# The token half of a Fourier mix as four 32-row products of even and odd tokens

## The chip, the cores and the metric

One core of a Trainium2 chip runs the whole kernel. The metric is the time on the device in microseconds; the median of several runs counts. Everything is float32.

## The reference

Attention inside chunks of 64 tokens, then a Fourier mix over tokens and channels, and a two-layer MLP on the normed sum:

```python
# q, k, v: (8, 8, 576, 64); chunk = 64
attn = softmax(q_c @ k_c.T / 8)            # in each of the 9 chunks of a head
x = (attn @ v_c) -> (8, 576, 512)          # heads side by side
mixed = real(fft(fft(x, axis=1), axis=2))  # over 576 tokens, then 512 channels
u = x + mixed
un = (u - mean(u)) / sqrt(var(u) + 1e-6)   # over the channels
out = u + relu(un @ w_ch1) @ w_ch2         # 512 -> 2048 -> 512; weights in float64
```

## The kernel before

**Tiles.** The 9 chunks of a batch of 576 tokens are held in tiles of 128 rows: `lo` tiles (chunks 0 to 3, tokens turned round), `hi` tiles (chunks 8 to 5, in mirrored order beside them), and a `rest` tile with chunk 4 of two batches, 64 rows each. NM = 2 pairs of lo and hi tiles, NQ = 289 outputs of the token transform, HQ = 128 channels, CH = 64.

**The mix.** The transform of a real signal folds in both directions. `fold` (L491) adds mirrored tokens (lo + hi) and mirrored channels, and leaves in `pm` four blocks T of 128 channels for each pair and a `pm_rest` for chunk 4, with one more column for the middle channel (L528). `fourier` (L644) then does the token half: `product` (L650) multiplies each block by the table `tk` (cosine or sine) into four PSUM tiles `z` (two of the pool `ps_t`, two called `more_z` of `ps_a`). For each T there are two products over 128 rows and one over 64 rows (`pm_rest`), each 289 columns wide, and twelve of one row of output for the middle channel. ACT copies the outputs to `zf` (tokens 0 to 255) and `zr` (the rest, mirrored; L678 to L688). `mixed` (L691) does the channel half with the tables ce, co, cx, so; `both` and `added` put the result back into the token tiles, mirrored. Batch 0 has its own `fourier_early` (L727), and `turn_tables` (L248) makes its tables in the wanted order from those in `start`.

**Order.** The order on each engine is written by hand. The main loop (L1212 to L1246) runs the MLP of group g as a generator (`mlp`, L1133): `up` steps and then `down` steps, each of 4 matmuls of 512 columns or 8 to 16 of 256. After each step t it advances the side work of the next batch, `attention(b)`, PAUSE = 3 empty steps, and `fourier(b)` (L1186). How many side steps are due is worked out from `sizes` (L1196), so that the batch is ready when its own MLP begins:

```python
due = min(sizes[cur], (t - t0) * sizes[cur] // (t1 - t0))
while done < due:
    heavy = next(sides[cur], None) or heavy
```

If no side step was `heavy`, `round_next` turns a piece of the weights from float64 to float32 on DVE and ACT (`round_weight`, L287), in group 0 only. `keep2` and `keep1` (L905, L888) then form sums of weight blocks on DVE and POOL and write them to DRAM (`s1`, `s2`), from where `fetch` (L926) brings them back for `up_halves` and `down_halves`. `operands` (L937) forms sums of h1.

**Queues.** SP issues nearly all DMAs in the order of the program: weights, q, k, v, the parts of s1 and s2, `shift` (L477: it moves single rows between tiles), and `store` (L871), which writes a finished tile to `out`.

Of the kernel before, what the change touches and what calls it, by code (L numbers as in the profile page):

```python
# [16 lines left out]
def kernel(  # L17
# [67 lines left out]
    tk = const.tile([128, NM + 1, 2, NQ], FP32, name="tk")  # L85
# [84 lines left out]
    more_v = one_p.tile([128, 4 * NL + 64], FP32, tag="zf", name="more_v")  # L170
# [53 lines left out]
    def load_tables():  # L224

        t = start[:, 0:(NM + 1) * 2 * NQ].rearrange("p (i r f) -> p i r f", i=NM + 1, r=2)
        for c in range(2 * NM):  # L230
            (i, r0), (j, p0) = divmod(c * CH, 128), divmod((NC - 1 - c) * CH, 128)
            nc.sync.dma_start(out=t[r0:r0 + CH, i], in_=seq_tab[p0:p0 + CH, j])
        for r0 in (0, CH):
            nc.sync.dma_start(out=t[r0:r0 + 1, NM], in_=seq_tab[0:1, 0])
            nc.sync.dma_start(out=t[r0 + 1:r0 + CH, NM], in_=seq_tab[1:CH, NM])
        for i in range(2):
            nc.sync.dma_start(out=first_rest[32 + 32 * i:33 + 32 * i, 0:DM], in_=dim_tab[0:1, 1 + 2 * i, :])
# [9 lines left out]

    def turn_tables():  # L248
        t = start[:, 0:(NM + 1) * 2 * NQ]
        a, b = tk.rearrange("p i r f -> p (i r) f"), t.rearrange("p (i f) -> p i f", f=NQ)  # L250
        for c in range(2 * NM):
            nc.scalar.copy(a[:, :, c * CH:(c + 1) * CH], b[:, :, (c + 1) * CH:c * CH:-1])
        nc.scalar.copy(a[:, :, NL:NL + 1], b[:, :, 0:1])
        nc.scalar.copy(a[:, :, NL + 1:NQ], b[:, :, NL + 1:NQ])
# [157 lines left out]
    def att_P(n):  # L412
        ex = es.pop(n)
        pt = turn(lambda j: ex[:, j].rearrange("p e k -> p (e k)"))
        t = one_p.tile([128, NJ, 128], FP32, tag="pT", name="pT")
        nc.scalar.copy(t, pt)
        pT[n] = t
# [45 lines left out]

    def shift_early(i):

        lows = [xt(at[LO, 0, j])[:, 0:DM] for j in range(NM)]
        rest, kept = xt(rests[0])[0:1, 0:DM], first_rest[0:1, 0:DM]
        if i == 0:
            nc.gpsimd.tensor_copy(kept, lows[1][0:1])
            nc.gpsimd.tensor_copy(lows[1][0:1], lows[1][CH:CH + 1])  # L470
            nc.gpsimd.tensor_copy(lows[1][CH:CH + 1], rest)
        else:
            nc.scalar.copy(rest, lows[0][0:1])
            nc.scalar.copy(lows[0][0:1], lows[0][CH:CH + 1])
            nc.scalar.copy(lows[0][CH:CH + 1], kept)

    def shift(b):  # L477

        lows = [xt(at[LO, b, i]) for i in range(NM)]
        r = b % 2 * CH  # L480
# [3 lines left out]
        for i in range(NM):  # L484
            eng.dma_start(out=t[2 * i:2 * i + 2, 0:DM], in_=lows[i][0:CH + 1:CH, 0:DM])
        eng.dma_start(out=t[2 * NM:2 * NM + 1, 0:DM], in_=rest)
        for i in range(NM):
            eng.dma_start(out=lows[i][0:CH + 1:CH, 0:DM], in_=t[2 * i + 1:2 * i + 3, 0:DM])
        eng.dma_start(out=rest, in_=t[0:1, 0:DM])

    def fold(b, i):  # L491
# [7 lines left out]
        if i < NM:  # L499
            pm = two_p.tile([128, DM + 1], FP32, tag="pm", name="pm")  # L500
# [5 lines left out]
        else:  # L506
            pm = two_p.tile([128, 2 * HQ + 1], FP32, tag="pm_rest", name="pm_rest")
# [10 lines left out]
        if i < NM:  # L518
# [3 lines left out]
            to = pm[:, 3 * HQ:DM + 1:HQ]  # L522
        else:
            for T, op in enumerate((ALU.add, ALU.subtract, ALU.subtract, ALU.add)):
                to = pm[T % 2 * CH:T % 2 * CH + CH, T // 2 * HQ:T // 2 * HQ + HQ]
                eng.tensor_tensor(out=to, in0=near[:, T // 2], in1=far[:, T // 2], op=op)
            to = pm[CH:, HQ:2 * HQ + 1:HQ]
        eng.tensor_copy(to, two[p, HM + 1 + HQ:HQ - 1:-HM - 1])  # L528
        pms[b, i] = pm

    def attention_early():
# [33 lines left out]
        turn_tables()  # L565
# [77 lines left out]

    def fourier(b):  # L644
        h = b % 2
        zf = one_p.tile([128, 4 * NL + 64], FP32, tag="zf", name="zf")
        zf = zf[:, 0:4 * NL].rearrange("p (t f) -> p t f", t=4)
        pm = [pms.pop((b, i)) for i in range(NM + 1)]

        def product(T, i, out_, lhsT, start, stop, cols=slice(0, NQ)):  # L650
            p = slice(0, 128) if i < NM else slice(T % 2 * CH, T % 2 * CH + CH)
            nc.tensor.matmul(  # L652
                out=out_, lhsT=lhsT[p], rhs=tk[p, i, T // 2 if T != 5 else 0, cols],
                start=start, stop=stop, skip_group_check=True,
            )


        z = [ps_t.tile([128, 512], FP32, tag="pt", name="z") for _ in range(2)]
        more = ps_a.tile([128, 2, 512], FP32, tag="att", name="more_z")
        z += [more[:, k] for k in range(2)]  # L660
        for T in range(4):
            for i in range(NM):
                product(T, i, z[T][:, 0:NQ], pm[i][:, T * HQ:(T + 1) * HQ], i == 0, False)
            if T == 1:
                yield
        for T in range(4):
            product(T, NM, z[T][:, 0:NQ], pm[NM][:, T // 2 * HQ:(T // 2 + 1) * HQ], False, True)

        mids = []
        for g, c0 in enumerate(range(0, NQ, NS)):  # L670
            c1 = min(c0 + NS, NQ)
            mids.append((c0, c1, z[2][32 * g:32 * g + 1, NQ:NQ + c1 - c0]))
        for i in range(NM + 1):
            for c0, c1, out_ in mids:
                one = pm[i][:, DM:DM + 1] if i < NM else pm[i][:, 2 * HQ:2 * HQ + 1]
                product(5, i, out_, one, i == 0, i == NM, slice(c0, c1))
        for T in range(4):
            nc.scalar.copy(zf[:, T, :], z[T][:, 0:NL])  # L678
            nc.scalar.copy(zr[:, T, h, 0:NQ - NL], z[T][:, NL:NQ])
            upper, mirrored = zr[:, T, h, NQ - NL:CH], z[T][:, NQ - 2:NL:-1]  # L680
            nc.scalar.activation(out=upper, in_=mirrored, func=ACTF.Copy, scale=1.0 if T < 2 else -1.0)
            for c0, c1, from_ in mids if T == 2 else ():
                n = max(0, min(c1, NL) - c0)
                if n > 0:
                    nc.scalar.copy(zf[0:1, T, c0:c0 + n], from_[:, 0:n])
                if c1 > NL:
                    nc.scalar.copy(zr[0:1, T, h, 0:NQ - NL], from_[:, n:])
                    nc.scalar.copy(zr[0:1, T, h, NQ - NL:CH], from_[:, NQ - 2 - c0:NL - c0:-1])  # L688
        yield
# [37 lines left out]
    def fourier_early():  # L727
# [3 lines left out]
        zf = one_p.tile([128, 4 * NL + 64], FP32, tag="zf", name="zf")  # L731
# [6 lines left out]
        mids = [(c0, min(c0 + NS, NQ)) for c0 in range(0, NQ, NS)]  # L738
        order = (1, 0, NM)
        for i in order:  # L740
            at_ = {"start": i == order[0], "stop": i == order[-1], "skip_group_check": True}
            for T in range(4):
                p = slice(0, 128) if i < NM else slice(T % 2 * CH, T % 2 * CH + CH)
                d0_ = T * HQ if i < NM else T // 2 * HQ
                nc.tensor.matmul(out=z[T][:, 0:NQ], lhsT=pm[i][p, d0_:d0_ + HQ], rhs=tk[p, i, T // 2], **at_)
            p, d0_ = (slice(0, 128), DM) if i < NM else (slice(CH, 128), 2 * HQ)
            for r, (c0, c1) in enumerate(mids):
                nc.tensor.matmul(
                    out=mid[32 * r:32 * r + 1, 0:c1 - c0], lhsT=pm[i][p, d0_:d0_ + 1], rhs=tk[p, i, 0, c0:c1], **at_
                )  # L750
        for T in range(4):
            if T % 2:
                nc.vector.tensor_copy(zf[:, T, :], z[T][:, 0:NL])
            else:
                nc.scalar.copy(zf[:, T, :], z[T][:, 0:NL])
        for r, (c0, c1) in enumerate(mids):
            n, from_ = min(c1, NL) - c0, mid[32 * r:32 * r + 1]
            if r % 2:
                nc.vector.tensor_copy(zf[0:1, 2, c0:c0 + n], from_[:, 0:n])
            else:  # L760
                nc.scalar.copy(zf[0:1, 2, c0:c0 + n], from_[:, 0:n])
        round_weight(1, put_off, "h")
        for T in range(4):
            nc.scalar.copy(zr[:, T, 0, 0:NQ - NL], z[T][:, NL:NQ])
            upper, mirrored = zr[:, T, 0, NQ - NL:CH], z[T][:, NQ - 2:NL:-1]
            nc.scalar.activation(out=upper, in_=mirrored, func=ACTF.Copy, scale=1.0 if T < 2 else -1.0)
            if T == 2:
                n = NL - c0
                nc.scalar.copy(zr[0:1, T, 0, 0:NQ - NL], from_[:, n:c1 - c0])
                nc.scalar.copy(zr[0:1, T, 0, NQ - NL:CH], from_[:, NQ - 2 - c0:n:-1])  # L770
# [100 lines left out]
    def store(n, o):  # L871

        if kind(n) == LO:
            b, c = chunks(n)[0]
            to = out[b, c * CH + 1:c * CH + 129, :].rearrange("(c p) d -> c p d", c=2)
            nc.sync.dma_start(out=to[:, ::-1], in_=o)
            return
        for h, (b, c) in enumerate(chunks(n)):
            r0, t0 = h * CH, c * CH
            if kind(n) == RE:  # L880
                eng = nc.scalar if n in groups[-1][1::2] and h else nc.sync
                eng.dma_start(out=out[b, t0 + 1:t0 + CH, :], in_=o[r0 + 1:r0 + CH])
                eng.dma_start(out=out[b, 0:1, :], in_=o[r0:r0 + 1])
            else:
                nc.sync.dma_start(out=out[b, t0:t0 + CH, :], in_=o[r0:r0 + CH])
# [253 lines left out]
    with tc.manual_schedule():  # L1139
        nc.vector.memset(warm, 0.0)  # L1140
        make_identity(nc, ident)
        nc.vector.memset(eps, 1e-6)
# [153 lines left out]
```

## Time and profile before

| | |
|---|---|
| median of 3 runs | 1090.54 us (1087.76 to 1090.62) |
| span of the profiled execution | 1089.0 us, from its first to its last instruction |
| TensorE (PE) busy | 1070.4 us |
| VectorE (DVE), ScalarE (ACT), GpSimd (POOL) busy | 577.2, 299.2, 280.3 us |
| mean granted clock of TensorE | 0.998 |
| DMA | 192.73 MB, mean 177 GB/s |

The profile has no time of its own for the profiled execution beside the span; it is set beside the runs above. A row of the profile gives start, length, engine, line, operation, tiles, shape and count; in brackets, how long the engine sat idle before and what ended that. PEld is the load of a matmul's stationary operand. A float32 matmul leaves two records.

### The profile page before, as it was taken

To read this page: it belongs to the slowest core of one execution; us is meant where nothing else is said; L and a number is where in the kernel's file an instruction comes from. 1 tells how busy PE (TensorE), PEld (TensorE's weight loads), DVE (VectorE), ACT (ScalarE), POOL (GpSimd) and SP (SyncE) were. 2 spreads that over 40 slices of the span, in tenths; PEclk is the share of its full clock that TensorE was granted. 3 is DMA by queue.
4 is the path that set the end of the run, shared out by engine and by line. 5 is a ranking of instruction groups with operands and counts; after the bars stand their busy time and mean duration, and the time that the engine had idled before them with its cause. 6 is when DMAs were issued, how large, how long until landed. Compare 5 with 4: busy or idle time off the path is not lost.

```text
span 1089.0 us, 18837 instructions
## 1 busy us (share of the span) xinstructions
PE 1070.4 (98%) x7018; PEld 848.7 (78%) x7018; DVE 577.2 (53%) x1258; ACT 299.2 (27%) x730; POOL 280.3 (26%) x403
## 2 busy tenths in 40 slices
PE   8999999999999999999999999999999999999998
PEld 6644454446888888888888888888888888888887
DVE  4899987314566355663556455735663534323411
ACT  4788453222113310322022212321133103101300
POOL 4301002444405140153114220514051401210140
PEclk9999999999999999999999999999999999999999
DMA  7777556679575637692668357854653455446232
GB/s 167 224 222 175 158 162 227 171 239 308 178 203 167 198 136 206 189 255 95 191 184 253 124 165 223 206 170 152 197 185 90 147 190 163 120 154 211 78 116 78
DMA packets 147970, 192.73 MB, mean 177 GB/s; under 512 B 66126, under 2 KB 104014, under 8 KB 140712
## 3 DMA queue, kind: packets, MB, share of 16 engines
q1 hardware_dynamic: 145620, 190.20, 58.4%
q8 instruction: 56, 0.92, 0.4%
q0 software_dynamic: 512, 0.68, 0.3%
q10 hardware_dynamic: 1748, 0.66, 0.2%
q14 instruction: 34, 0.28, 0.1%
HBM read 167.22 MB, written 24.12 MB: 176 GB/s over the span
## 4 chain that ended last, share of the span: by engine, by line
PE 89%; DVE 4%; ACT 2%; DMA 2%; SPq 2%; issue 1%; POOL 0%; DVEq 0%; ACTq 0%
PE pb L1089 20%; PE pa L1040 17%; PE pa L1089 15%; PE pb L1040 13%; PE up L973 4%; PE up L953 3%; PE pt L333 3%; PE dn L994 3%; PE mix L700 2%; PE sc L384 2%; PE more_z L652 2%; PE xp L432 2%; PE z L652 1%; PE idle L1167 1%; DMA xall<-in_moe_w_ch_dram 1%; SPq L195 1%
## 5 line engine op out<-in xcount | busy, mean ns | idle before, releaser
L1040 PE MATMUL pa<-unT,wa 128*128 128x256 f32 x672 | 159.5, 380 | 1.1 <-DVE wa L1048 1.1
L1040 PEld LDWEIGHTS pa<-unT,wa 128*128 128x128 f32 x672 | 126.5, 190 | 18.9 <-DVE wa L1048 1.5
L941 POOL TENSOR_TENSOR h<-h 128x256 f32<-128x256 f32 x64 | 55.7, 877 | 269.5 <-PE pb L1040 150.5
L1089 PE MATMUL pa<-wb,h 128*128 128x256 f32 x512 | 115.6, 380 | 0.0
L1089 PE MATMUL pb<-wb,h 128*128 128x256 f32 x512 | 114.9, 379 | 0.0
L1040 PE MATMUL pb<-wa 128*128 128x256 f32 x448 | 106.6, 381 | 0.0
L1089 PEld LDWEIGHTS pa<-wb,h 128*128 128x128 f32 x512 | 96.1, 190 | 13.5 <-issue 0.5
L1089 PEld LDWEIGHTS pb<-wb,h 128*128 128x128 f32 x512 | 96.3, 190 | 12.6
L1040 PEld LDWEIGHTS pb<-wa 128*128 128x128 f32 x448 | 84.2, 190 | 11.6 <-DVE h L1056 0.2
L994 PE MATMUL dn<-wb,h 128*128 128x512 f32 x128 | 58.4, 605 | 0.9 <-ACT h L964 0.9
L1046 DVE TENSOR_TENSOR wa<-pb,wa 128x256 f32<-128x256 f32 x56 | 23.5, 423 | 65.5 <-ACT wa L1045 65.5
L1089 PE MATMUL pb<-wb,yall 128*128 128x256 f32 x256 | 58.2, 381 | 0.0
L1089 PE MATMUL pa<-wb,yall 128*128 128x256 f32 x256 | 57.9, 380 | 0.0
L1089 PE MATMUL pb<-wb 128*128 128x256 f32 x256 | 57.7, 379 | 0.0
L973 PE MATMUL up<-unT,wa 128*128 128x512 f32 x128 | 56.8, 596 | 0.0
L1045 ACT COPY wa<-pa 128x256 f32<-128x256 f32 x56 | 20.8, 372 | 125.1 <-PE pa L1040 125.1
L1040 PE MATMUL pa<-wa 128*128 128x256 f32 x224 | 53.5, 382 | 0.0
L717 POOL TENSOR_TENSOR xall<-y,xall 128x513 f32<-128x513 f32 x14 | 21.3, 1518 | 125.3 <-DVE y L711 125.3
L1040 PE MATMUL pb<-unT,wa 128*128 128x256 f32 x224 | 52.9, 379 | 0.0
L1089 PEld LDWEIGHTS pa<-wb,yall 128*128 128x128 f32 x256 | 47.7, 190 | 6.4
L1089 PEld LDWEIGHTS pb<-wb,yall 128*128 128x128 f32 x256 | 47.7, 190 | 6.3
L1089 PEld LDWEIGHTS pb<-wb 128*128 128x128 f32 x256 | 47.6, 190 | 5.9
(250 smaller groups left out, 1685.0 us busy)
## 6 DMA issues: line engine op xcount, KB each, us to landing
wb<-s SPq DMA_DIRECT2D x56, 1024.0 KB
wa<-s SPq DMA_DIRECT2D x196, 256.0 KB
xall<-in_moe_w_ch_dram SPq DMA_DIRECT2D x22, 512.0 KB
q<-in_q_dram SPq DMA_DIRECT2D x96, 112.0 KB
k<-in_k_dram SPq DMA_DIRECT2D x96, 112.0 KB
v<-in_v_dram SPq DMA_DIRECT2D x124, 64.0 KB
yall<-in_moe_w_ch_dram SPq DMA_DIRECT2D x10, 512.0 KB
s<-wb SPq DMA_DIRECT2D x20, 256.0 KB
```

What stands on the lines that cost most here:

```text
L333: nc.tensor.transpose(pt[:, j, :], src(j), ident)
L384: nc.tensor.matmul(out=sc[t0:t0 + CH, e, j * CH:(j + 1) * CH], lhsT=a[r0:r0 + D, 2 * j + c, 0:CH], rhs=b[r0:r0 + D, 2 * j + c, 0:CH], star ...
L432: nc.tensor.matmul(out=xp[0][e][t0:t0 + CH, j * DV:(j + 1) * DV], lhsT=a[r0:r0 + CH, j, t0:t0 + CH], rhs=b[r0:r0 + CH, c, j, :], start=Tru ...
L652: nc.tensor.matmul(out=out_, lhsT=lhsT[p], rhs=tk[p, i, T // 2 if T != 5 else 0, cols], start=start, stop=stop, skip_group_check=True,)
L700: nc.tensor.matmul(out=mix[:, cols], lhsT=zt[:, T], rhs=tab, start=(T == 0), stop=(T == 3), skip_group_check=True,)
L941: nc.gpsimd.tensor_tensor(out=h1[:, m, hi], in0=h1[:, m, lo], in1=h1[:, m, hi], op=ALU.subtract)
L953: nc.tensor.matmul(out=up, lhsT=w1[:, kk, m * 128:(m + 1) * 128], rhs=unT[:, kk], start=(kk == 0), stop=(kk == KD - 1), skip_group_check=True,
L973: nc.tensor.matmul(out=up, lhsT=w1[:, kk, m * 128:(m + 1) * 128], rhs=unT[:, kk], start=(kk == 0), stop=(kk == KD - 1),)
L994: nc.tensor.matmul(out=dn, lhsT=h1[:, m, s * 128:(s + 1) * 128], rhs=w2[:, m, :], start=(m == 0), stop=(m == KF - 1),)
L1040: nc.tensor.matmul(out=dst, lhsT=w[:, kk, r], rhs=rhs[o][:, kk], start=(o in (0, 1) and kk == 0), stop=(kk == 1), skip_group_check=True,)
L1046: nc.vector.tensor_tensor(out=b, in0=pbs[r][:, 0], in1=a, op=ALU.add)
L1089: nc.tensor.matmul(out=dst, lhsT=lhs[:, m], rhs=w[:, m], start=(o in (0, 2) and m == 0), stop=(m == HF - 1), skip_group_check=True,)
```

## The change

The tokens of a chunk are held 32 odd ones first, then 32 even ones. The token transform is done for outputs 0 to 144 only (NE = NQ // 2 + 1 = 145), for odd and even tokens apart; outputs above 144 follow from the same products, as even minus odd parts (for the sine, odd minus even).

- `z_sets` does 8 matmuls of 32 rows and 145 columns, one for each 32-row part and each of two blocks; a batch has five such sets, three in its first step (both pairs and the rest), two in its second, with the halves of the rows swapped against each other. Four 32-row parts write to four PSUM banks.
- `mid_products` does the middle channel in two halves of 73 and 72 columns, for a plain and a signed column (`sign`, in `fold`), eight in the first step and four in the second; one element of it is copied out by ACT in between.
- `z_odd` (ACT) copies the odd part, `z_joined` (DVE) forms sum and differences in a new tile `zs`, `z_tile` and `z_rest` (ACT) bring them into the order of the tiles.
- `fourier` has one more step for batches above 1, and `sizes` one more; for batch 1 two steps are called heavy.
- Batch 0 keeps its products of 128 rows and 289 columns, from the tables in `start`; `turn_tables` goes. `token_tables` loads the tables in odd and even order, once for batch 0 and once for the rest.
- `att_P` writes pT in the new order of tokens; `shift` and `shift_early` take rows 32 and 96 where they took 0 and 64.
- `store` writes each half of a chunk with a stride of two rows: for hi tiles one half from SP and one from ACT.

```diff
-    tk = const.tile([128, NM + 1, 2, NQ], FP32, name="tk")
+    NE = NQ // 2 + 1
+    tk = const.tile([128, NM + 1, 2, NE], FP32, name="tk")
...
+    def token_tables(to):
+        n = to.shape[-1]
+        for c in range(2):
+            j, p0 = divmod((NC - 1 - c) * CH, 128)
+            for r in range(2):
+                r0 = CH * c + CH // 2 * r
+                nc.sync.dma_start(
+                    out=to[r0:r0 + CH // 2, 0:NM].rearrange("p i r f -> p (i r) f"),
+                    in_=seq_tab[p0 + 1 - r:p0 + CH:2, j - NM + 1:j + 1, :, 0:n].rearrange("p i r f -> p (i r) f"),
+                )
...
-        nc.scalar.copy(t, pt)
+        nc.scalar.copy(
+            t.rearrange("p j (c r i) -> p (j c) r i", c=2, r=2), pt.rearrange("p j (c i r) -> p (j c) r i", c=2, r=2)[:, :, ::-1]
+        )
...
         eng.tensor_copy(to, two[p, HM + 1 + HQ:HQ - 1:-HM - 1])
+        eng.tensor_tensor(out=pm[rows, m0 + 1:m0 + 2], in0=pm[rows, m0:m0 + 1], in1=sign[rows], op=ALU.mult)
...
-        turn_tables()
...
+    def z_sets(z, pm, i, turn_, first=False):
+        for s in range(2):
+            for q_ in range(4):
+                k, r = (q_ // 2 + turn_) % 2, q_ % 2
+                T, p = 2 * k + s, slice(32 * q_, 32 * q_ + 32)
+                d0_ = T * HQ if i < NM else s * HQ
+                nc.tensor.matmul(
+                    out=z[r][k][:, s * NE:(s + 1) * NE], lhsT=pm[i][p, d0_:d0_ + HQ],
+                    rhs=tk[p, NM - 1 - i if i < NM else NM, k],
+                    start=first and s == 0, stop=False, skip_group_check=True,
+                )
...
+    def z_odd():
+        for k in range(2):
+            nc.scalar.copy(zs[0][:, 2 * k:2 * k + 2, 1], zs[2][k][:, 0:2 * NE].rearrange("p (t f) -> p t f", t=2))
+
+    def z_joined():
+        even = zs[1][:, :, 0:2 * NE].rearrange("p k (t f) -> p k t f", t=2)
+        z4 = zs[0].rearrange("p (k t) r f -> p k t r f", t=2)
+        nc.vector.tensor_tensor(out=z4[:, :, :, 0], in0=even, in1=z4[:, :, :, 1], op=ALU.add)
+        for k in range(2):
+            e, o = even[:, k], z4[:, k, :, 1]
+            a, b = (e, o) if k == 0 else (o, e)
+            nc.vector.tensor_tensor(out=o, in0=a, in1=b, op=ALU.subtract)
...
     def fourier(b):
...
+        z = z_space()
         for i in range(NM + 1):
+            z_sets(z, pm, i, 0, i == 0)
+        outs = [z[0][0][32 * g:32 * g + 1, 2 * NE:] for g in range(4)]
+        for i in range(NM):
+            mid_products(outs, pm, i)
+        nc.scalar.copy(middle[:, 0, 0:1], outs[0][:, 0:1])
+        yield b == 1
+        mid_products(outs, pm, NM)
+        for i in range(NM):
+            z_sets(z, pm, i, 1)
+        z_middle(outs)
+        z_odd()
+        if b == 1:
+            z_joined()
+        else:
+            yield
+            z_joined()
+        nc.scalar.copy(zs[0][0:1, 2], middle)
+        if h == 1:
+            z_rest(h)
+        for i in range(NM):
+            z_tile(zf, i)
+        if h == 0:
+            z_rest(h)
+        yield b == 1
...
             else:
-                nc.sync.dma_start(out=out[b, t0:t0 + CH, :], in_=o[r0:r0 + CH])
+                for r in range(2):
+                    eng = nc.scalar if r else nc.sync
+                    eng.dma_start(out=out[b, t0 + 1 - r:t0 + CH:2, :], in_=o[r0 + ODD * r:r0 + ODD * r + ODD])
...
+        token_tables(tk)
         PAUSE = 3
...
-            sizes.append((4 * n_tiles + 1 if b == 1 else 3 * n_tiles + 1) + PAUSE + 2 + NM + b % 2)
+            sizes.append((4 * n_tiles + 1 if b == 1 else 3 * n_tiles + 1) + PAUSE + 2 + (b > 1) + NM + b % 2)
```

## The prediction

> **What bounds the kernel now.** I read the page's busy times first, then the chain of waits, then the token transform on TensorE in order of time, then the waits around batches 1 and 2.
>
> ```profile
> PE 1070.4 (98%) x7018; PEld 848.7 (78%) x7018; DVE 577.2 (53%) x1258; ACT 299.2 (27%) x730; POOL 280.3 (26%) x403
> PE 89%; DVE 4%; ACT 2%; DMA 2%; SPq 2%; issue 1%; POOL 0%; DVEq 0%; ACTq 0%
> ```
>
> TensorE is busy 1070.4 of 1089.0 us and carries 89% of the chain: a microsecond of matmul taken away is won, unless something else is due at that point. Per batch the transform (L652) costs this (chain of waits in order of time, then TensorE alone; each fp32 matmul is two records):
>
> ```profile
> 367.36 1.95 PE z L652 x8
> 371.03 1.95 PE more_z L652 x8
> 374.75 7.11 PE pa L1089 x32
> ```
>
> ```profile
> 370.87 2.11 PE L652 MATMUL more_z<-tk,pm 128*128 128x289 f32 x8
> 372.91 0.76 PE L652 MATMUL z<-tk,pm_rest 64*128 64x289 f32 x4
> 373.50 0.66 PE L652 MATMUL more_z<-tk,pm_rest 64*128 64x289 f32 x4
> 374.08 0.43 PE L652 MATMUL more_z<-tk,pm 128*1 128x73 f32 x16
> 374.44 0.30 PE L652 MATMUL more_z<-tk,pm_rest 64*1 64x73 f32 x8
> 374.68 1.56 PE L1089 MATMUL pa<-wb,h 128*128 128x256 f32 x6
> ```
>
> Four full matmuls take 1.95 us: 0.4875 us per 289 columns, 1.69 ns a column. The batch takes 1.95 + (374.75 - 371.03) = **5.67 us**, seven times (1 to 7). The four 64-row matmuls take 374.08 - 372.91 = 1.17 us where 4 x 0.4875 = 1.95 would be serial: two row halves run at once (0.975) and 0.195 goes to the change of shape. The 128x1 and 64x1 groups take 0.36 and 0.24 us against 0.246 and 0.123 us when four columns run at once: 0.115 each for the change.
>
> **What the Trainium skill says.** "TensorE: Matmul & The Clock Gate", Part 3, says matmuls in different 32-row groups run together, 3.07 times faster for four; its section "LDWEIGHTS (loading the stationary operand)" says a 32-row load takes as long as a 128-row one. The trace agrees for halves: loads of 64x128 take 188 ns, of 128x128 190 ns, yet the pairs overlap. No 32-row part is in it. "TensorEngine Tiling (Array Packing)", Key Properties, says changing the tiling drains the array: the 0.115 to 0.195 us above. Part 1 of the first page says an idle TensorE has its clock halved; the trace shows 0.54 granted from 153.8 to 157.3 us, after a stall.
>
> **The change, part by part** (sum against the profiled span, 1089.0; the median of the runs is 1090.54, so 1.5 us lie around it).
>
> 1. *Token matmuls, batches 1 to 7.* Removed: 8 of 128x289 and 4 of 64x289. Added: 40 of 32x145 in five sets of 8; four row groups write four banks. If four run at once, a set is two waves of 145 x 1.69 = 0.245 us, 0.49 us. Step one: three sets 1.47 + 0.195, eight one-column matmuls 0.36. Step two: four such 0.24, two sets 0.98 + 0.195. Two returns to full shape at 0.1. Sum **3.64 us**, so 2.03 saved, x7 = **-14.2**. Bounds: changes free, 2.8 us (-20); 0.4 each, 5.2 us (-3). Weight loads must hide: 64 columns take 134 ns, 128 take 190, so some 112 ns of a 128-column load repeat per row group, under the 122 ns that one record streams.
>
> 2. *Copies and joins.* ACT's 18 copies per batch become some 16 over 290 to 256 columns; DVE gets three sums, 580 + 290 + 290 elements, 0.77 + 2 x 0.45 = 1.7 us (0.69 per 512 from the rows of L399). For even batches the chain is: z_odd 0.7, sums 1.7, then ACT after its copy of pa (3.9 us after the last product), `middle` and z_tile to 5.7; mix comes 6.9 us after, behind two blocks of 8 matmuls (3.45 each). Odd batches from 3 have 8.6 us. Nothing; if that cover went, each late microsecond would cost three. more_z is held a step longer; the next scores, which use its PSUM, come after the mixes. POOL's sign products (0.19 x3) end 12 us before z in batches 3 to 7. Nothing.
>
> 3. *Stores.* Per batch SP issues 8 instead of 6 (0.3 to 0.6 us each), ACT 4. ACT waits there for DVE's last sum of the `down`; behind it stands a copy of pT, which has 3.45 us of matmul. Nothing. At the very end ACT issues three where it issued two: +0.3.
>
> 4. *First batch.* turn_tables goes (six copies, 29.65 to 31.77), but TensorE is in idle matmuls to 31.70: nothing. zr takes 15 short ACT copies for 10, 0.11 each, before rstd at 41.86: **+0.4** (0 to +1). The second table load puts 10 DMAs, about 4.5 us, on SP near 53 us, behind v; weight pieces are loaded several ahead. Nothing (0 to +2).
>
> 5. *Batch 1.* Now ACT's z copies queue behind weight rounding:
>
> ```profile
> 151.47 0.35 ACT L678 COPY zf<-z 128x256 f32<-128x256 f32 x1
> ...
> 152.06 0.49 PE L700 MATMUL mix<-ce,zr 128*128 128x129 f32 x2 [1.12 <-ACT zr L681]
> ...
> 153.82 1.22 PE L700 MATMUL mix<-cx,zr 128*128 128x256 f32 x2 [0.82 <-ACT zr L688]
> ```
>
> dn would have gone on at 147.24 + 3.44 + 0.9 = 151.6; it does at 155.3, with 1 us of slow clock to come: 4.7 lost. After: two steps skip the rounding (`yield b == 1`), but `mid_products` of the rest rows must wait for the new 1x1 copy on ACT, behind the rounding that ends at 145.4. TensorE is there at about 143.2: 2.3 us, then 0.2 for mix and 1.6 of slow clock. Net **-0.6** (-4 to +2).
>
> 6. *Batch 2.* This is what I trust least. Its pm has no slack today:
>
> ```profile
> 244.07 0.53 DVE L939 TENSOR_TENSOR wb<-h 128x256 f32<-128x256 f32 x1 [13.82 <-DMA s<-wb]
> ...
> 249.83 1.11 DVE L352 STREAM_TRANSPOSE kT<-k 128x512 f32<-128x512 f32 x1 [2.96 <-DMA k<-in_k_dram]
> ...
> 251.57 0.22 DVE L445 TENSOR_SCALAR rd<-xp 128x4 f32<-128x4 f32 x2
> ```
>
> POOL's fold follows at 252.6 and ends at 257.7; z starts at 257.31. The source is SP, which issues weight parts, q, k, v and stores with hardly a gap from 183 us on. The change makes side steps of b > 1 one more, so z of batch 2 stands one step earlier: directly behind the `up` block that ends at 253.9. TensorE, 2.6 us ahead, is there at 251.3. SP isn't ahead: DVE's weight parts (L916) come after the put-off rounding, some 10 us later, two more stores are issued, but the 3.7 us that SP waited near 204 may be absorbed. I take pm 1 us earlier, 256.7: TensorE waits 5.4 us, plus 0.8 (half a chance of the 1.6 of slow clock): **+6.2** (0 to +11). Batches 4 and 6 move a step or two earlier too, but have pm 12 us ahead.
>
> Sum: -14.2 + 0.4 - 0.6 + 6.2 + 0.3 = **-7.9**; span 1081.1, median about **1082.5**.
>
> **The rivals.** (a) *No stall in batch 2*: SP catches up and all of step 1 arrives: 1090.5 - 14.1 = **1076** (1072 to 1079). For it: SP's gaps before 183. Against: a DMA on the chain at 224 us. (b) *Only two row groups at once*: a set costs 0.98; 4.9 + 0.37 + 0.82 = 6.09 us, +0.42 x7 = +2.9, and little stall: **1093**. For it: no trace here has four. Against: quadrants of scores (32 records of 64x64 in 0.47 us, 15 ns each, in the chain at 198.95) already run four at a time, two rows by two columns. (c) *Slower: weight loads serialize.* If 16 loads of a set queue at 112 ns, it costs 1.79 us; 5 x 1.79 + 0.37 + 0.82 = 10.1 us, +4.5 x7 = +31: **1122**. It decides above (5.67 - 1.19) / 80 = 56 ns per load. Against: the scores' 64-column loads, 56 ns each by the same slope, follow each other at 15 ns. (d) *SP later still*, 5 us more in batch 2 or a stall moved into its attention: 1087 to 1092. That the matmuls aren't tiled as written is excluded by their row slices, 32 apart.
>
> **How the numbers follow.** Likeliest 0.52 (1078 to 1087), (a) 0.25, (b) 0.08, (c) 0.05, (d) 0.10. Anything within 0.3%, 1087.3 to 1093.8, is about what a measurement here can't tell from no change. Faster: 0.52 + 0.25 and a little of (d), 0.78; same: most of (b) and (d), 0.14; slower: (c) and the rest, 0.08. The range 1073 to 1089 leaves out (b), (c) and half of (d).
>
> **What would show it.** Right: L652's 5.67 us become 3.4 to 4 us with z, more_z in 32*128 forms, four overlapping; a wait of TensorE for pm in batch 2 near 250 us; PE busy about 1056. Wrong: sets above 0.9 us (b, c); no wait at batch 2 (a); waits of mix for zf in even batches, which would break step 2.

## Result: 1150.14 us, slower by 5.4%, and the profile after

The changed kernel takes **1150.14 us** (median of 4 runs, 1147.59 to 1152.92) where the kernel before takes 1090.58: a ratio of **1.0544** (95% interval 1.0518 to 1.0569), 59.6 us more. The forecast was 1082.5, range 1073 to 1089. The profiled execution has a span of 1148.8 us at a granted clock of 0.974 (before 0.998). Its page, busy times and chain:

```profile
PE 1073.1 (93%) x7410; PEld 847.8 (74%) x7410; DVE 587.6 (51%) x1287; ACT 307.9 (27%) x729; POOL 283.8 (25%) x423
PE 71%; DMA 5%; issue 2%; DVE 2%; SPq 2%; POOL 2%; ACT 1%; DVEq 0%; POOLq 0%; ACTq 0%
```

TensorE's share of the chain went from 89% to 71%, and DMA's from 2% to 5%. TensorE is idle for 1148.8 - 1073.1 = 75.7 us, against 18.6 before. It is busy no less than before although it has less to do, because it runs at a lower clock behind its long waits: 0.50 was granted from 125 to 132 us, 0.64 from 235 to 250 us.

**The transform itself does what it should.** Batch 3 on TensorE in order of time (start, length, line, tiles):

```profile
402.32 0.39 PE L666 MATMUL z<-tk,pm 32*128 32x145 f32 x1
...
402.54 0.28 PE L666 MATMUL z<-tk,pm 32*128 32x145 f32 x1
402.55 0.28 PE L666 MATMUL more_z<-tk,pm 32*128 32x145 f32 x1
...
404.01 0.43 PE L676 MATMUL z<-tk,pm 128*1 128x73 f32 x16
404.37 1.99 PE L1137 MATMUL pa<-unT,wa 128*128 128x256 f32 x8
...
408.02 0.30 PE L676 MATMUL z<-tk,pm_rest 64*1 64x73 f32 x8
...
409.45 0.92 PE L1137 MATMUL pa<-unT,wa 128*128 128x256 f32 x3
```

The first step lasts from 402.32 to 404.37, the second from 408.02 to 409.45: 2.05 + 1.43 = **3.48 us**, where the old transform took 5.67. Seven batches save 15.3 us.

**The time goes in waits elsewhere.** TensorE's longest waits after the change (who, for whom, total us, times, longest):

```profile
PE sc L391 <- DVE rd L454: 12.2, 2, 10.3
PE pa L1137 <- DVE wa L1145: 12.1, 4, 4.1
PE dn L1091 <- ACT h L1061: 9.7, 1, 9.7
PE pb L1137 <- DMA wa<-s: 5.7, 3, 3.0
PE pt L340 <- ACT un L937: 3.7, 3, 2.1
```

The two longest in total before, where no single wait was above 1.4 us:

```profile
PE sc L384 <- ACT kT L372: 1.7, 2, 1.0
PE sc L384 <- DVE rd L445: 1.4, 1, 1.4
```

The same points of the two traces give the course of the loss (us):

| point | before | after | later by |
|---|---|---|---|
| first turn of `un` for the MLP | 43.71 | 48.79 | 5.1 |
| first xp after group 0's first `dn` | 123.58 | 139.84 | 16.3 |
| xp of batch 2's first tile | 182.37 | 198.80 | 16.4 |
| z of batch 3 | 367.19 | 402.32 | 35.1 |
| z of batch 5 | 598.39 | 642.55 | 44.2 |
| z of batch 7 | 827.90 | 875.07 | 47.2 |
| DVE's last sum | 1084.32 | 1132.86 | 48.5 |
| end of the span | 1089.0 | 1148.8 | 59.8 |

(z stands some steps earlier among the MLP's steps, so those rows are good to about 3.5 us.) The table has four stretches: the start (5), one wait near 119 us (11), the loop from 199 us on (32, with 13 us of the transform's saving inside), and the end (11).

**Near 119 us.** DVE, POOL and TensorE, and last TensorE at the same point of the kernel before:

```profile
118.67 0.43 DVE L315 TENSOR_SCALAR wb<-xall 128x512 uint32<-128x512 uint32 x1 [9.36 <-DMA xall<-first]
...
112.65 1.07 POOL L500 DMA_DIRECT2D xall<-first  x2 [1.99 <-issue]
...
128.38 2.07 PE L1091 MATMUL dn<-wb,h 128*128 128x512 f32 x2 [9.73 <-ACT h L1061]
...
114.51 3.70 PE L994 MATMUL dn<-wb,h 128*128 128x512 f32 x8 [0.94 <-ACT h L964]
```

DVE stands still for 9.36 us before a weight piece, until the shift of batch 1 has written rows 32 and 96 back; ACT's rounding and its copy of h queue behind, TensorE waits 9.73 us. In the program of the kernel before, the same instruction waits for its weight piece alone, and its trace has no such stop.

**Batch 2's attention** (DVE, SP, TensorE):

```profile
221.66 0.76 DVE L458 TENSOR_TENSOR xall<-xp,rd 128x256 f32<-128x256 f32 x2 [9.17 <-DMA s<-xall]
238.38 1.08 DVE L359 STREAM_TRANSPOSE kT<-k 128x512 f32<-128x512 f32 x1 [13.60 <-DMA k<-in_k_dram]
...
221.64 1.31 SPq L972 DMA_DIRECT2D out_dram<-o  x2
223.05 2.67 SPq L980 DMA_DIRECT2D out_dram<-o  x2
225.82 2.01 SPq L972 DMA_DIRECT2D out_dram<-o  x2
227.92 2.80 SPq L980 DMA_DIRECT2D out_dram<-o  x2
230.82 2.41 SPq L198 DMA_DIRECT2D k<-in_k_dram  x4
...
239.52 1.13 PE L391 MATMUL sc<-kT,qT 64*64 64x64 f32 x32 [10.34 <-DVE rd L454]
```

DVE first waits for kept weights to leave xall. Then it stands still for 13.6 us before k, which SP issues behind eight stores.

**The MLP blocks of four groups.** SP issues stores between the loads there, and TensorE waits for a `wa` in each, at 368 and 374, 489 and 495, 611 and 616, and 735 us. An example from 476 us on (SP, DVE, TensorE):

```profile
476.56 1.02 SPq L980 DMA_DIRECT2D out_dram<-wb  x2
...
479.39 1.76 SPq L198 DMA_DIRECT2D q<-in_q_dram  x4
485.57 2.70 SPq L198 DMA_DIRECT2D k<-in_k_dram  x4
...
487.30 1.09 DVE L359 STREAM_TRANSPOSE qT<-q 128x512 f32<-128x512 f32 x1 [4.24 <-DMA q<-in_q_dram]
493.20 1.08 DVE L359 STREAM_TRANSPOSE kT<-k 128x512 f32<-128x512 f32 x1 [4.23 <-DMA k<-in_k_dram]
494.13 0.73 DVE L1145 TENSOR_TENSOR wa<-pa,wa 128x256 f32<-128x256 f32 x2
...
494.59 3.39 PE L1137 MATMUL pa<-unT,wa 128*128 128x256 f32 x8 [3.90 <-DVE wa L1145]
```

The line that TensorE names, `wa`, is a DVE sum without a fault of its own: it stands in DVE's order behind the turn of k, and k is late. Over the run DVE waits 41.1 + 37.5 us for q and k; before it was 12.3 + 21.4.

**The end** (DVE and ACT, and last DVE's last sum in the kernel before; then what the DMA engines moved from 1140 to 1149 us, in 40 slices):

```profile
1132.86 0.42 DVE L1206 TENSOR_TENSOR wb<-pb,wb 128x256 f32<-128x256 f32 x1 [3.10 <-PE pb L1186]
...
1135.62 0.34 ACTq L975 DMA_DIRECT2D out_dram<-wb  x1
...
1139.19 0.54 ACTq L982 DMA_DIRECT2D out_dram<-wb  x1
...
1084.32 0.42 DVE L1109 TENSOR_TENSOR wb<-pb,wb 128x256 f32<-128x256 f32 x1 [3.10 <-PE pb L1089]
```

```profile
GB/s 27 36 18 27 27 27 27 18 27 27 27 27 18 27 27 27 27 18 27 27 27 18 27 27 27 27 18 27 27 27 18 0 0 0 0 0 0 0 0 0
```

DVE is done at 1133.28, the span ends 15.5 us later; before it was 4.3 us (DVE's last sum ended at 1084.74, the span at 1089.0). ACT gets its first store out 2.3 us late, its last at 1139.19, and the remaining rows then trickle out at some 25 GB/s: the packets in the trace, a row of 2 KB each, start 80 ns apart, those of SP's and ACT's queue in turn. The Trainium skill says why, on "DMA: Bandwidth & Descriptors", section "Why a DMA increments its semaphore by 16 and not by 1": a DMA issued by SP or ACT runs on the largest number of engines up to 16 that divides the slowest dimension of both patterns. A rest tile's even rows are now 31 rows, a prime, so by that rule one engine carries them, and the single file of packets agrees. The 63 rows of before divide by 9. A high store of 32 rows would run on 16 engines and a low store, whose pattern begins with a dimension of 2, on 2. By the same section each engine that takes part marks its end once on the DMA's semaphore: SP's and ACT's 918 DMAs left 13643 such marks in the trace, the rule gives 13612, and 16 for each would be 14688.

### The profile page after: what moved, and what is told of

Its sections match the earlier page's. It is cut to its first block, busy times and chain, and to the rows that moved or that the text cites. A ratio compares the mean times of both kernels' runs of the same rounds, so it can differ in the third digit from the quotient of the medians.

```text
span 1148.8 us, 19798 instructions
## 1 busy us (share of the span) xinstructions
PE 1073.1 (93%) x7410; PEld 847.8 (74%) x7410; DVE 587.6 (51%) x1287; ACT 307.9 (27%) x729; POOL 283.8 (25%) x423
## 4 chain that ended last, share of the span: by engine, by line
PE 71%; DMA 5%; issue 2%; DVE 2%; SPq 2%; POOL 2%; ACT 1%; DVEq 0%; POOLq 0%; ACTq 0%
PE pb L1186 18%; PE pa L1137 15%; PE pa L1186 15%; PE pb L1137 11%; PE up L1070 3%; PE pt L340 2%; DMA q<-in_q_dram 2%; PE mix L783 1%; PE z L666 1%; DMA out_dram<-wb 1%; DMA k<-in_k_dram 1%; PE xp L441 1%; SPq L198 1%; PE sc L391 1%; PE dn L1091 1%
## 5 line engine op out<-in xcount | busy, mean ns | idle before, releaser
L1137 PE MATMUL pa<-unT,wa 128*128 128x256 f32 x672 | 165.2, 390 | 12.1 <-DVE wa L1145 12.1
L1137 PEld LDWEIGHTS pb<-wa 128*128 128x128 f32 x448 | 85.6, 193 | 12.3
L1137 PE MATMUL pb<-unT,wa 128*128 128x256 f32 x224 | 56.2, 396 | 7.1 <-DMA wa<-s 5.7
L1070 PE MATMUL up<-unT,wa 128*128 128x512 f32 x128 | 59.3, 618 | 0.0
L1186 PE MATMUL pa<-wb,yall 128*128 128x256 f32 x256 | 57.6, 379 | 0.0
L1151 ACT ACTIVATE h<-pa 128x256 f32<-128x256 f32 x56 | 21.5, 383 | 134.6 <-PE pa L1137 124.5
L1137 PEld LDWEIGHTS pb<-unT,wa 128*128 128x128 f32 x224 | 43.7, 197 | 15.1 <-issue 6.2
L1143 DVE TENSOR_TENSOR wa<-pb,wa 128x256 f32<-128x256 f32 x56 | 23.5, 423 | 59.4 <-ACT wa L1142 59.4
L1137 PE MATMUL pa<-wa 128*128 128x256 f32 x224 | 52.9, 379 | 0.0
```

What stands on the lines that cost most here:

```text
L1070: nc.tensor.matmul(out=up, lhsT=w1[:, kk, m * 128:(m + 1) * 128], rhs=unT[:, kk], start=(kk == 0), stop=(kk == KD - 1),)
L1137: nc.tensor.matmul(out=dst, lhsT=w[:, kk, r], rhs=rhs[o][:, kk], start=(o in (0, 1) and kk == 0), stop=(kk == 1), skip_group_check=True,)
L1143: nc.vector.tensor_tensor(out=b, in0=pbs[r][:, 0], in1=a, op=ALU.add)
L1151: nc.scalar.activation(out=h1[:, m, lo], in_=dst, func=ACTF.Relu)
L1186: nc.tensor.matmul(out=dst, lhsT=lhs[:, m], rhs=w[:, m], start=(o in (0, 2) and m == 0), stop=(m == HF - 1), skip_group_check=True,)
```

## The experiments

All times are medians; ratios are to the kernel before on the same chip, with 95% intervals. A gain written as a product with 1091 us is a difference of two ratios, for runs on different chips; the others are differences of medians.

| run | us | ratio |
|---|---|---|
| changed kernel | 1150.14 | 1.0544 (1.0518 to 1.0569) |
| e1_old_stores | 1132.35 | 1.0381 (1.0360 to 1.0401) |
| e2_new_stores (in the kernel before) | 1115.21 | 1.0225 (1.0206 to 1.0245) |
| e3_single_rows | 1142.90 | 1.0476 (1.0453 to 1.0499) |
| e4_sp_alone | 1156.30 | 1.0590 (1.0564 to 1.0616) |
| e5_mended | 1131.15 | 1.0369 (1.0344 to 1.0395) |
| e6_mended_as_before_paused | 1113.74 | 1.0209 (1.0180 to 1.0237) |
| e7_mended_no_skip | 1125.42 | 1.0315 (1.0288 to 1.0342) |
| e8_mended_both | 1109.04 | 1.0174 (1.0146 to 1.0201) |
| e9_low_stores_pool | 1090.58 | 0.9995 (0.9981 to 1.0009) |
| e10_high_stores_pool | 1092.22 | 1.0018 (1.0006 to 1.0030) |
| **e11_all_stores_pool** | **1083.55** | **0.9939 (0.9923 to 0.9954)** |
| e12_changed_stores_pool | 1116.88 | 1.0259 (1.0242 to 1.0276) |
| e13_mended_stores_pool | 1095.51 | 1.0047 (1.0031 to 1.0064) |
| e14_before_stores_pool (the kernel before) | 1087.08 | 0.9973 (0.9963 to 0.9983) |

### Stores or order?

**e1_old_stores**: the changed kernel with the old `store`. **e2_new_stores**: the kernel before with the new one. Both leave the rows of `out` in another order than the reference.

```diff
# e1; e2 is the reverse, in the kernel before
     def store(n, o):
-        last = n in groups[-1][1::2]
...
+        if kind(n) == LO:
+            b, c = chunks(n)[0]
+            to = out[b, c * CH + 1:c * CH + 129, :].rearrange("(c p) d -> c p d", c=2)
+            nc.sync.dma_start(out=to[:, ::-1], in_=o)
+            return
...
+                nc.sync.dma_start(out=out[b, t0:t0 + CH, :], in_=o[r0:r0 + CH])
```

> The changed kernel with the store function of the kernel before (one 128-row DMA per low tile, two 64-row ones per high tile, 63 + 1 rows for the rest rows, SP alone but for the end); rows of the output so land in another token order than the reference's. Theory S (the stores): 12 store DMAs a batch instead of 6, some of them on few DMA engines, hold up the loads behind them on SP and ACT's queue. Then most of what goes after the first 180 us comes back: 1150 - 11 (the end) - 20 (the waits for k, wa and wb around the stores) = 1119, 1112 to 1126. Rival O (the order): the waits around batch 2 and the pa blocks come from the transform's steps standing earlier and from the skipped rounding. Then only the end comes back: 1139, 1136 to 1142.

> The kernel before with the store function of the changed one alone; tokens stay in their old order on chip, so rows of the output land in another token order than the reference's. Theory S: 1090 + 11 + 20 = 1121, 1112 to 1130, with PE waiting for wa and for k as in the changed kernel. Rival O: the end alone, 1101, 1098 to 1104.

Measured: e1 1132.35, between the two bands; e2 1115.21, inside that of theory S. In e1's trace the end is 4.6 us long again (DVE's last sum to the end), z of batch 7 stands 8.1 us earlier (867.02), but the waits of `pa` for `wa` are all there:

```profile
PE pa L1134 <- DVE wa L1142: 13.0, 4, 3.5
PE sc L391 <- DVE rd L454: 12.0, 2, 10.0
PE dn L1088 <- ACT h L1058: 10.0, 1, 10.0
```

So neither theory explains it alone. The new stores cost 24.5 us in the kernel before (0.0225 x 1091), 11.4 of it at the end (15.7 us from DVE's last sum instead of 4.3), and yet the old ones leave the changed kernel 41 us behind: something else costs time too.

### The strided write-back

**e3_single_rows**:

```diff
         for i in range(NM):
-            eng.dma_start(out=lows[i][LONE, 0:DM], in_=t[2 * i + 1:2 * i + 3, 0:DM])
+            for h in range(2 if b == 1 else 0):
+                to = lows[i][ODD + CH * h:ODD + CH * h + 1, 0:DM]
+                eng.dma_start(out=to, in_=t[2 * i + 1 + h:2 * i + 2 + h, 0:DM])
+            if b > 1:
+                eng.dma_start(out=lows[i][LONE, 0:DM], in_=t[2 * i + 1:2 * i + 3, 0:DM])
```

> The changed kernel, with the write-back of rows 32 and 96 in the shift of batch 1 as one DMA per row instead of one DMA with a step of 64 rows (POOL issues 5 writes instead of 3). Theory W: the 9.4 us in which DVE waits for xall<-first before it may round a weight piece comes from that strided write standing for all columns between its rows in the program's waits; with single rows the wait is gone, the dn block starts at about 119 instead of 128, and 9.7 + 2.4 us (slow clock) come back: 1138, 1134 to 1142. Rival: the weight piece itself lands late (SP's queue), the wait stays under another name, 1149 to 1152.

Measured: 1142.90, 7.2 us less, just short of the band (1134 to 1142). The wait is gone from DVE's list, and the dn block starts where W said:

```profile
118.64 1.55 PE L1095 MATMUL dn<-wb,h 128*128 128x512 f32 x3 [0.94 <-ACT h L1065]
```

The waits of that one DVE instruction in the program, for DMAs of SP and ACT (DMAHW) and of POOL (DMASW), in the changed kernel and then in e3:

```
183 L315 TensorScalarPtr wb_93<-xall_97 128x512 [waits DMAHW2_49,DMASW6_49,DMASW5_49]
183 L315 TensorScalarPtr wb_93<-xall_97 128x512 [waits DMAHW2_49]
```

The piece lies in other columns of xall than the shifted rows. The waits for POOL's writes are in the program with the write of rows 32 and 96 at once, and not with single rows. The step of 64 rows isn't enough for them: the kernel before writes rows 0 and 64 with the same step, and this instruction waits for one DMAHW alone there. Theory W holds: TensorE's wait of 9.73 us at this point is 0.94, and 7.2 us of it are left in the whole, since batch 2's attention still waits (8.6 us).

### Is it ACT?

**e4_sp_alone**: in the changed kernel ACT's copy `wa<-pa` waits 38.3 us in all, four times, behind ACT's own stores; here SP issues these.

```diff
-                    eng = nc.scalar if r else nc.sync
+                    eng = nc.sync
```

> The changed kernel with the odd rows' stores of the high tiles issued by SP instead of ACT. Theory S says that a store is held by the DMA eight before it and holds the one eight after, whoever issues it: SP's queue gets 4 more, ACT's copy of pa is free; 1145, 1138 to 1150. Rival A (ACT alone is the trouble: its queue stands behind its stores and holds the copy wa<-pa): all four waits of pa for wa, 12.1 us, and the slow clock after them, some 6, go: 1132, 1128 to 1136.

Measured: 1156.30, some 5 us slower than the changed kernel (0.0046 x 1091; the two intervals just overlap), against both expectations. Rival A is out: ACT no longer waits for its stores, and TensorE's waits of `pa` for `wa` are 13.9 us. The reading that fits is that ACT had shared SP's load and that SP's queue is the tight one; neither theory had that in its number.

### The end, the tables, the side steps and the skips

**e5_mended** is e3 without 31-row DMAs:

```diff
-                eng.dma_start(out=out[b, t0 + 2:t0 + CH:2, :], in_=o[r0 + ODD + 1:r0 + CH])
+                eng.dma_start(out=out[b, t0 + 2:t0 + ODD + 2:2, :], in_=o[r0 + ODD + 1:r0 + ODD + 17])
+                eng.dma_start(out=out[b, t0 + ODD + 2:t0 + CH:2, :], in_=o[r0 + ODD + 17:r0 + CH])
...
-            nc.sync.dma_start(out=to[r0 + CH // 2 + 1:r0 + CH, NM], in_=seq_tab[2:CH:2, NM, :, 0:n])
+            for r1, m in ((1, 16), (17, 15)):
...
```

**e6_mended_as_before_paused** and **e7_mended_no_skip** add one edit each to e5, **e8_mended_both** adds both:

```diff
# e6
-            for _ in range(PAUSE):
+            for _ in range(PAUSE - (b > 1)):
...
-            sizes.append((...) + PAUSE + 2 + (b > 1) + NM + b % 2)
+            sizes.append((...) + PAUSE + 2 + NM + b % 2)
# e7, twice
-        yield b == 1
+        yield
```

> The changed kernel with the single rows of e3_single_rows and no DMA of 31 rows: the rest rows' even stores go as 15 or 16 rows each instead of 31, the 31-row table loads as 16 + 15. Theory E (a 31-row DMA moves on one DMA engine, row after row at 80 ns, and the DMA eight places on waits for it): from the last matmul to the end of the span takes 6 us as with e1_old_stores instead of 16; SP no longer waits 2.5 us for a table before its weight pieces, so the first un is turned 2 us earlier. Against e3's 1143: 1131, 1127 to 1135. Rival (the number of stores holds the end, not their shape): there is one more store per chunk now, so 1143 to 1146.

> e5_mended, with one pause step less ahead of the transform in batches 2 to 7, so that a batch has as many side steps as in the kernel before and its attention's steps stand where they stood. Theory D (the side steps stand closer together by one, so two tiles' q and k are wanted too soon after each other; SP loads each only after DVE has turned the one before): the eight waits of 1 to 4.5 us of pa and pb for wa, 20 us in all, and a part of the slow clock behind them go: 1131 - 18 = 1113, 1108 to 1120. Rival S (they come of the stores in SP's and ACT's queues): they stay, 1128 to 1132.

> e5_mended without the skipped rounding: batch 1's two transform steps no longer keep the step's weight rounding back. Theory K: those skips make the rounding, and with it the sums and stores of the kept weights in xall, end later, DVE's first tile of batch 2 waits 9.7 us for s<-xall, k's loads are issued behind it and the stores, and TensorE waits 8.6 us for rd at 228 and 1.8 at 245. Without them these go, 12 us with the clock, and 2 to 3 come back in batch 1, where the copy to middle stands behind the rounding: 1131 - 9 = 1122, 1118 to 1126. Rival D or S: the wait at 228 stays, 1131 to 1134.

> e5_mended with both: one pause step less in batches 2 to 7 and no skipped rounding. If theories D and K hold apart from each other, both gains add: 1131 - 18 - 9 = 1104, 1098 to 1110, with what is left the stores in the loop. If one lateness of SP is behind both, the sum is less: 1108 to 1116. If the stores are behind both (S): 1128 to 1134.

Measured: 1131.15 (expected 1131), 1113.74 (1113), 1125.42 (1122, in the band), 1109.04 (1104, in the band). Apart, e6's and e7's edits gain 17.4 and 5.7 us, together 22.1, so they nearly add.

- Theory E: with one store *more* per rest chunk, the end is nearly as short as in e1 (5.7 us for 4.6), so the shape holds the end and not the number. DVE's last sum in e5, and e5's DMA from 1122 to 1130 us:

```profile
1123.46 0.42 DVE L1214 TENSOR_TENSOR wb<-pb,wb 128x256 f32<-128x256 f32 x1 [3.10 <-PE pb L1194]
```

```profile
GB/s 82 62 82 205 51 123 41 102 51 0 0 21 0 82 205 277 154 103 0 113 41 0 20 41 103 21 123 31 0 0 0 0 0 0 0 0 0 41 0 0
```

The same bytes come in bursts of up to 277 GB/s, and the span ends 5.7 us after DVE instead of 15.5. The tables gave some 1.6 us for 2 expected: the first turn of `un` lies at 47.55 to 48.79 us in the five traces with the 31-row pieces of the first table (mean 48.20) and at 45.76 to 47.30 us in the eight without (mean 46.62).

- Theory D: one side step less per batch takes 17 us. TensorE's waits of `pa` for `wa` go from 13.0 us (in e5) to 6.9, and the mean granted clock rises from 0.980 to 0.987, some 8 us of the span; the wait of batch 2 stays:

```profile
PE sc L394 <- DVE rd L457: 10.9, 1, 10.9
PE pa L1145 <- DVE wa L1153: 6.9, 4, 2.2
PE pb L1145 <- DMA wa<-s: 4.1, 2, 2.6
```

- Theory K: without the skips DVE's wait for `s<-xall` (9.1 us in e5) is gone, and half of batch 2's wait with it. What stays is k behind the stores:

```profile
220.17 1.08 DVE L362 STREAM_TRANSPOSE kT<-k 128x512 f32<-128x512 f32 x1 [13.04 <-DMA k<-in_k_dram]
...
221.31 1.14 PE L394 MATMUL sc<-kT,qT 64*64 64x64 f32 x32 [4.41 <-DVE rd L457]
```

### The stores' own queue

A completion semaphore is a counter that a DMA raises when its data have landed. In these programs SP and ACT share eight of them, taken in turn, and every DMA waits for the one eight places earlier to have landed. Three of SP's instructions in the program of the changed kernel, each with the next semaphore:

```
L221 DMACopy v0_99<-in_v_dram 64x4x64 [waits DMAHW3_49,PE_49]
L221 DMACopy v0_99<-in_v_dram 64x4x64 [waits DMAHW4_49,PE_49]
L221 DMACopy v0_99<-in_v_dram 64x4x64 [waits DMAHW5_49]
```

A batch now stores with 12 DMAs instead of 6. The following runs give e8's stores to POOL, whose DMAs have eight semaphores of their own:

```diff
# e9
-                nc.sync.dma_start(out=to, in_=o[r0:r0 + CH])
+                nc.gpsimd.dma_start(out=to, in_=o[r0:r0 + CH])
# e10
-                    eng = nc.scalar if r else nc.sync
+                    eng = nc.gpsimd
# e11: both
```

> e8_mended_both with the four low stores of a batch (64 rows each, falling order) issued by POOL instead of SP. Theory R: these are the slow ones, 2 DMA engines carry them, and what SP issues behind them (q, k, wa) shares [...]the turn of eight with them; on POOL they have their own. The waits of pa and pb for wa and of sc for rd near the stores, some 15 us with the clock, fall by half to two thirds: 1109 - 9 = 1100, 1095 to 1104. Rival C (count, not shape: each of the 12 stores costs SP or ACT a place): a third of it, 1104 to 1108. Rival P: POOL's sums h stand behind stores that wait for DVE, 1109 to 1116.

> e8_mended_both with the eight high stores of a batch (32 rows each, 16 DMA engines) issued by POOL instead of SP and ACT. Theory R: they are fast, only their places in the turn of eight come free: 1109 - 4 = 1105, 1102 to 1109. Rival C: two thirds of the gain are here, 1097 to 1102. Rival P: 1109 to 1118, POOL has twice as many issues as in e9.

> e8_mended_both with all twelve stores of a batch from POOL (the rest rows at the end stay on SP and ACT). Theories R and C alike: what the stores cost in the loop is gone, 1109 - 14 = 1095, 1090 to 1100. Rival P: 1108 to 1120, with TensorE or DVE waiting for POOL's h, or for pm in batch 2.

Measured: 1090.58, 1092.22 and 1083.55, all faster than expected. Either part alone is worth 17 to 20 us, both 25.6 (0.0235 x 1091): shape (R) and count (C) don't decide it. Moving the stores takes three things from SP at once, and its issues and waits, as the traces put them down, tell them apart (us):

| SP's time | before | changed | e8 | e9 | e10 | e11 | e14 (below) |
|---|---|---|---|---|---|---|---|
| issuing stores | 35.3 | 40.2 | 39.8 | 22.2 | 26.8 | 8.2 | 3.3 |
| at a store, until the sum that it writes is ready | 68.4 | 48.6 | 53.3 | 57.6 | 34.6 | 11.8 | 17.5 |
| at any DMA, until an earlier store has landed | 23.9 | 70.7 | 52.9 | 23.5 | 23.3 | 3.7 | 2.2 |

```profile
SPq L980 <- DMA out_dram<-wb: 20.3, 10, 3.5
```

(The line is the largest part of the 70.7.) The issue and the wait for the sum, two rivals that no run tests alone, were about as large or larger in the kernel before, and taking both from it (e14) gains 2.8 us. The wait for landing is what the change tripled, and e9 and e10 each bring it back to the level of before. Rival P is out: POOL is 31% busy in e11, and no wait of TensorE is put down to it. TensorE's list in e8 and then in e11:

```profile
PE pa L1145 <- DVE wa L1153: 8.0, 4, 3.6
PE sc L394 <- DVE rd L457: 5.0, 1, 5.0
PE mix L790 <- ACT zr L739: 3.7, 1, 3.7
```

```profile
PE mix L790 <- ACT zr L739: 3.8, 1, 3.8
PE z L683 <- ACT middle L760: 1.7, 1, 1.7
PE pt L343 <- ACT un L944: 1.6, 2, 1.1
```

What is left is batch 1's wait behind the weight rounding. DVE waits for q and k 4.5 + 12.0 us in e11, less than in the kernel before. **e11 is faster than both kernels**, than the kernel before by 0.6%; the interval leaves out 1.

### Which of these costs stand alone?

**e12** is the changed kernel with e11's two edits alone, **e13** is e5 with them, **e14** the kernel before with its loop stores on POOL (`nc.sync` to `nc.gpsimd` in two lines).

> The changed kernel with nothing else than its low and high stores on POOL; the strided write-back, the 31-row DMAs, the pause and the skips stay. Theory J (the pause and the skips cost only because SP is late, and the stores make it late): what stays is the wait for the shift's rows, 12 us, the end, 10, and the tables, 2: 1083.5 + 24 = 1107, 1102 to 1112. Theory I (each costs by itself): 1150 - 25 = 1125, 1120 to 1130.

> e11_all_stores_pool with the pause and the skipped rounding as the changed kernel has them (e5_mended with low and high stores on POOL). Theory J: 1084, 1080 to 1089, a few us of batch 1's waits for zr gone and as much to pay in batch 2. Theory I: e5 stood 22 us above e8, so 1083.5 + 22 = 1105, 1100 to 1109.

> The kernel before with its low and high stores issued by POOL. If e11's gain is the transform's (15 us saved, some 8 of it lost again in batch 1 and at the start), the kernel before has little to win: its waits near stores are 1.4 + 1.1 us: 1090, 1087 to 1092. If the queue is what makes e11 fast: 1083 to 1086.

Measured: 1116.88, 1095.51 and 1087.08. Both J and I miss. The two edits of e11 gain some 31 us in the changed kernel itself (e12, 0.0285 x 1091), more than the 25.6 at the end of the mends. Pause and skip cost 22 us with the stores on SP and ACT (e5 to e8) and 12 with them on POOL (e13 to e11), so somewhat more than half is theirs and the rest is one lateness counted twice. e14 gains 2.8 us (by its interval 1.9 to 4.0), so the queue alone doesn't explain e11: against e14's ratio, e11's lies 0.34% lower, some 3.7 us, and the intervals don't meet. In the two traces e11 turns its first `un` 2.9 us later than e14, is 7.2 us behind at batch 2's first tile, 3.6 ahead at DVE's last sum and 2.5 ahead at the end. So of the 13.1 us that the transform saves in batches 2 to 7, some 10.8 arrive; the start and batch 1 cost 7.2 again, and the end 1.1.

## Why the prediction was wrong

**Step 1 (token matmuls) was right**, mechanism and size: 3.48 us for 3.64, 15.3 saved for 14.2. The records of one set start four abreast, 0.12 us a wave. One after the other they would need an estimated 16 x 0.1225 = 1.96 us (from 1.69 ns a column in the kernel before), so the four row groups ran about 4 times faster. The Trainium skill's page named there, "TensorE: Matmul & The Clock Gate", Part 3, says 3.07, and the measurement decides here. What is left of the 3.48 us is 0.11 for each of six changes of shape. The 32-row loads take 184 to 185 ns each and stay hidden. Rivals (b) and (c) are out.

**Step 2 (copies and joins) was right in what it put at nothing:** TensorE waits once before a `mix`, in batch 1 and for zr (1.05 us), and before none for zf.

**Step 3 (stores) failed, and cost the most, at its words "Nothing" and "At the very end ACT issues three where it issued two: +0.3".** The step counted issue times and asked who waits on ACT. It did not ask how long a store takes to land, nor who waits for that. The end cost 11.2 us, 9.8 of it the 31-row DMAs (15.5 to 5.7 us). In the loop the twelve stores on SP and ACT cost some 31 us in the changed kernel (e12) and 25.6 after the mends (e8 to e11). The wait behind landing stores tripled, from 23.9 to 70.7 us of SP's time.

**Step 4 (first batch): 5.1 us for 0.4.** Its "Nothing (0 to +2)" for the second table load looked at the wrong load: the 31-row pieces of the first one hold SP, weights arrive late, and the copies of z, which stand behind the rounding on ACT and DVE, with them. In the changed kernel DVE waits for a weight piece

```profile
38.54 0.43 DVE L315 TENSOR_SCALAR wa<-yall 128x512 uint32<-128x512 uint32 x1 [2.60 <-DMA yall<-in_moe_w_ch_dram]
```

and zf comes 1.35 us late for TensorE. The table pieces were worth some 1.6 us. Another 2.2 us are there by 20 us already (some 2.0 in the mean of the traces with the changed first batch), where TensorE waits for loads of k into `start` that the diff doesn't touch; their cause stays open, and so does the rest.

**A part that no step priced: the shift's rows.** Rows 32 and 96 for 0 and 64 looked like the same DMA. It cost TensorE 9.7 us and a stretch of slow clock at that point, 7.2 us of the whole (e3), by a wait whose reason only the program shows.

**Step 5 (batch 1): -0.6 expected.** `middle` was 1.88 us late for 2.3 forecast, zr 1.05 for 0.2, but TensorE also waited 2.07 us for un afterwards. So step 1's 2.2 us were used up, and the batch came out even (16.3 to 16.4 in the table).

**Step 6 (batch 2) had the right source and the wrong place.** SP is late, as it said, and rival (d) named the attention, but with 1087 to 1092; pm never stopped TensorE. The step priced the new order at z alone. The put-off rounding ("some 10 us later") moved the kept weights' way out of xall into batch 2's attention (e7). And "batches 4 and 6 move a step or two earlier too, but have pm 12 us ahead" is true of pm and beside the point: one more side step in `sizes` moves all of a batch's attention steps closer together, and its q and k, loaded one tile at a time through SP, are then late (e6, 17 us).

In sum: steps 3, 4 and 6 looked at the queue's issue time and at the product at the end of the chain. What decided was landing time, and every load behind. The mends gave in turn 7.2 (rows) + 11.8 (31 rows) + 22.1 (pause and skip) + 25.5 us (stores' queue) = 66.6, and 1150.1 - 66.6 = 1083.5. These are differences of one chain of runs, so they add up in any case; in another order the shares differ, as e12 and e13 show.

## What to carry to other kernels

Where one queue issues loads and stores, a change of a store's shape is to be priced by when it lands and by what stands behind it, not by its issue: count its rows, see what divides them, and look for the loads that follow. Before adding a step to a generator that spreads side work over a main loop, ask what each of its *other* steps then wants earlier. And a wait named after a healthy instruction (`wa`) is followed upward on that engine until something outside it, here k, is late.

## What was not expected of the hardware

- The stores' issuing engine was worth 25.6 us (e8 to e11) with the same bytes. The Trainium skill, "DMA: Bandwidth & Descriptors", section "Issuing engines are not separate DMA queues", says that other issuing engines only save the sequencer's time. Here SP's time for issuing stores fell by 31.6 us, and its time behind stores that hadn't landed by 49.2: in a program whose DMAs wait for each other in turn, the issuing engine also decides what waits for what. How much of the 25.6 us each of the two is worth, no run shows alone.
- The 31-row stores at the end moved at some 25 GB/s; split in 15 and 16 rows (e5), the same rows came in bursts of up to 277 GB/s.
- Moving 4 of 12 stores (e9) was worth 19.5 us, moving the other 8 (e10) 17, both 25.6: the gains don't add up. Each alone already brings SP's wait for landing stores back to the level of the kernel before, which fits.
